# Attention in front of a SiLU layer: full-array scores with zero-padded keys, values for four heads in 32-column tiles, q in 128 partitions

## The chip, the cores and the metric

The kernel runs on one core of a Trainium2 chip. The metric is device time in microseconds (us), the median of several executions of the same program. An execution counts as fast when it lies within 1.5% of the fastest of its kernel. Unless it says otherwise, everything below compares fast runs.

## The reference

Keys and values are averaged over groups of 8 positions, then ordinary attention is computed, and its result is fed to a two-layer network with SiLU.

```python
B, H, S, D = 8, 8, 576, 64                       # q, k, v, float32
k_p = k.reshape(B, H, 72, 8, D).mean(axis=3)      # 72 pooled keys
v_p = v.reshape(B, H, 72, 8, D).mean(axis=3)
attn = softmax(q @ k_p^T / sqrt(D))               # 576 x 72 per head
x = (attn @ v_p) as (4608 tokens, 512)
out = silu(x @ w_in) @ w_out                      # 512 -> 2048 -> 512
```

The inputs are drawn at 0.1 (q, k, v), so a score is a few thousandths and the softmax is nearly flat. That matters for one experiment below.

## The kernel before

There are nine passes of 512 tokens ("iterations" t). Each is `up` (64 matmuls into hp_ps, then SiLU) and `down` (64 matmuls into o_ps). The attention of batch t+1 is woven between the matmuls of iteration t. A "visit" is one pair of heads and half of the queries: two score matmuls, the exponential, two matmuls for the sums (den), two for the values (nu).

```python
# scores: 64 rows per head, the two heads on the two row halves
for s in range(2):
    rows = slice(s * D, (s + 1) * D)
    nc.tensor.matmul(sc_ps[:, s, :HS], lhsT=st["kT"][rows, p, :],
                     rhs=st[f"qT{p}"][rows, cols], start=True, stop=True)
# ... exponential on ScalarE ...
# sums and values: 64 columns per head
for s in range(2):
    nc.tensor.matmul(den_ps[s*D:(s+1)*D, :HS], lhsT=ones, rhs=es[:, s, :], ...)
for s in range(2):
    nc.tensor.matmul(nu_ps[s*D:(s+1)*D, :HS], lhsT=st["vp"][:, 2*p+s, :], rhs=es[:, s, :], ...)
# ... 1/den as exp(-ln(den)) on ScalarE ...
# xT is written with a step of 6 bf16 elements
dst = xT[:, p, b*S:(b+1)*S].rearrange("d (q j) -> d j q", j=QJ)
nc.vector.tensor_mul(out=dst[:, f*HJ:(f+1)*HJ, :], in0=nu_ps..., in1=rec...)

# loads: q in 96 partitions, k and v in 72; all on SyncE's queue
q_src = q[b].rearrange("h (p j) d -> p h (j d)", j=QJ)      # QJ = 6
k_src = k[b].rearrange("h (sp p) d -> sp h (p d)", p=POOL)
# ... weights on GpSimd's queue: w_in in 4 loads, then w_out in 4 loads
for c in range(NC):
    nc.gpsimd.dma_start(out=w_in_sb[:, :, cs], in_=w_in_r[:, :, cs])
```

Of the kernel before, what the change touches and what calls it, by code (L numbers as in the profile page):

```python
# [27 lines left out]
FP32 = mybir.dt.float32  # L28
FP32R = mybir.dt.float32r
BF16 = mybir.dt.bfloat16  # L30
# [6 lines left out]
def kernel(  # L37
# [9 lines left out]
    nc = tc.nc  # L47

    B, H, S, D = q.shape
    POOL = 8  # L50
    SP = S // POOL
# [8 lines left out]
    QP = 96  # L60
    QJ = S // QP
    HS = S // 2
    HJ = QJ // 2
    score_scale = float(1.0 / (D ** 0.5) / POOL)
    assert NT == B + 1 and NP == KF

    w_in_r = moe_w_in.rearrange("(kt kp) f -> kp kt f", kp=128)
    w_out_r = moe_w_out.rearrange("(kt kp) d -> kp kt d", kp=128)

# [10 lines left out]
    ones = singles.tile([SP, D], BF16, name="ones")  # L80
# [3 lines left out]

    batches = {}

    def load_batch(b, parts):
        st = batches.setdefault(b, {})
        k_raw = big.tile([SP, H, POOL * D], FP32, tag="k_raw", name="k_raw")
        q_raw = big.tile([QP, H, QJ * D], FP32, tag="q_raw", name="q_raw")  # L90
        v_raw = big.tile([SP, H, POOL * D], FP32, tag="v_raw", name="v_raw")
        st.update(k_raw=k_raw, q_raw=q_raw, v_raw=v_raw)
        k_src = k[b].rearrange("h (sp p) d -> sp h (p d)", p=POOL)
        v_src = v[b].rearrange("h (sp p) d -> sp h (p d)", p=POOL)
        q_src = q[b].rearrange("h (p j) d -> p h (j d)", j=QJ)
        hp = H // parts
        for i in range(parts):
            hs = slice(i * hp, (i + 1) * hp)
            nc.sync.dma_start(out=k_raw[:, hs, :], in_=k_src[:, hs, :])
            nc.sync.dma_start(out=q_raw[:, hs, :], in_=q_src[:, hs, :])  # L100
        for i in range(parts):
            hs = slice(i * hp, (i + 1) * hp)
            nc.sync.dma_start(out=v_raw[:, hs, :], in_=v_src[:, hs, :])

    def cast_q(b, parts):
        st = batches[b]
        q_bf = big.tile([QP, NP, QJ, 2, D], BF16, tag="q_bf", bufs=1, name="q_bf")
        st["q_bf"] = q_bf
        hp = H // parts
        for i in range(parts):  # L110
            for p in range(i * hp // 2, (i + 1) * hp // 2):
                for s in range(2):
                    nc.gpsimd.tensor_copy(  # L113
                        out=q_bf[:, p, :, s, :],
                        in_=st["q_raw"][:, 2 * p + s, :].rearrange(
                            "q (j d) -> q j d", d=D
                        ),
                    )

    def pool_kv(b, which, parts):  # L120
        st = batches[b]
        raw = st[f"{which}_raw"]
        dst = mid.tile([SP, H, D], BF16, tag=f"{which}p", name=f"{which}p")
        st[f"{which}p"] = dst
        hp = H // parts
        for i in range(parts):
            hs = slice(i * hp, (i + 1) * hp)
            w = POOL * D // 2
            while w > D:
                nc.vector.tensor_add(  # L130
                    out=raw[:, hs, :w], in0=raw[:, hs, :w], in1=raw[:, hs, w : 2 * w]
                )
                w //= 2
            nc.vector.tensor_add(  # L134
                out=dst[:, hs, :], in0=raw[:, hs, :D], in1=raw[:, hs, D : 2 * D]
            )

    def k_transpose(b):
        st = batches[b]
        kT_ps = psum.tile([128, NP, SP], BF16, tag="mm", bufs=3, name="kT_ps")  # L140
        for p in range(NP):
            nc.tensor.transpose(  # L142
                kT_ps[:, p, :],
                st["kp"][:, 2 * p : 2 * p + 2, :].rearrange("s h d -> s (h d)"),
                ident[:SP, :SP],
            )
        kT = mid.tile([128, NP, SP], BF16, tag="kT", name="kT")
        nc.vector.tensor_copy(out=kT, in_=kT_ps)
        st["kT"] = kT

    def q_transpose(b, p):
        st = batches[b]
        qT_ps = psum.tile([128, QJ, QP], BF16, tag="mm", bufs=3, name="qT_ps")
        for j in range(QJ):
            nc.tensor.transpose(  # L155
                qT_ps[:, j, :],
                st["q_bf"][:, p, j, :, :].rearrange("q s d -> q (s d)"),
                ident[:QP, :QP],
            )
        qT = mid.tile([128, S], BF16, tag=f"qT{p}", bufs=1, name="qT")  # L160
        nc.vector.tensor_copy(out=qT, in_=qT_ps.rearrange("d j q -> d (j q)"))  # L161
        st[f"qT{p}"] = qT

    def scores(b, p, f):
        st = batches[b]
        cols = slice(f * HS, (f + 1) * HS)
        sc_ps = psum.tile([SP, 2, 512], FP32, tag="sc", bufs=1, name="sc_ps")
        for s in range(2):
            rows = slice(s * D, (s + 1) * D)
            nc.tensor.matmul(  # L170
                sc_ps[:, s, :HS],
                lhsT=st["kT"][rows, p, :],
                rhs=st[f"qT{p}"][rows, cols],
                start=True, stop=True,
            )
        es = mid.tile([SP, 2, HS], BF16, tag="es", bufs=3, name="es")
        nc.scalar.activation(es, sc_ps[:, :, :HS], func=AF.Exp, scale=score_scale)  # L177
        st[f"es{p}{f}"] = es

    def values(b, p, f):  # L180
        st = batches[b]
        es = st.pop(f"es{p}{f}")
        nu_ps = psum.tile([128, 512], FP32, tag="nd", bufs=3, name="nu_ps")
        den_ps = psum.tile([128, 512], FP32, tag="nd", bufs=3, name="den_ps")
        for s in range(2):
            nc.tensor.matmul(  # L186
                den_ps[s * D : (s + 1) * D, :HS],
                lhsT=ones, rhs=es[:, s, :], start=True, stop=True,
            )
        for s in range(2):  # L190
            nc.tensor.matmul(  # L191
                nu_ps[s * D : (s + 1) * D, :HS],
                lhsT=st["vp"][:, 2 * p + s, :], rhs=es[:, s, :],
                start=True, stop=True,
            )
        lnd = mid.tile([128, HS], FP32, tag="lnd", name="lnd")
        nc.scalar.activation(lnd, den_ps[:, :HS], func=AF.Ln)  # L197
        rec = mid.tile([128, HS], FP32, tag="rec", name="rec")
        nc.scalar.activation(rec, lnd, func=AF.Exp, scale=-1.0)  # L199
        dst = xT[:, p, b * S : (b + 1) * S].rearrange("d (q j) -> d j q", j=QJ)  # L200
        nc.vector.tensor_mul(  # L201
            out=dst[:, f * HJ : (f + 1) * HJ, :],
            in0=nu_ps[:, :HS].rearrange("d (j q) -> d j q", q=QP),
            in1=rec.rearrange("d (j q) -> d j q", q=QP),
        )
# [37 lines left out]
    def down(t, h_T, fillers):  # L243
        nm = NTT // 128
        step = spread(fillers, nm * KG)
        for m in range(nm):
# [11 lines left out]
            r0 = t * NTT + m * 128  # L258
            nc.sync.dma_start(out=out[r0 : r0 + 128, :], in_=o_sb)
# [4 lines left out]
    load_batch(0, 2)  # L264
# [3 lines left out]
    cast_q(0, 2)  # L268
    NC = 4
    for c in range(NC):  # L270
        cs = slice(c * d_ff // NC, (c + 1) * d_ff // NC)
        nc.gpsimd.dma_start(out=w_in_sb[:, :, cs], in_=w_in_r[:, :, cs])  # L272
    for c in range(NC):
        cs = slice(c * KG // NC, (c + 1) * KG // NC)
        nc.gpsimd.dma_start(out=w_out_sb[:, cs, :], in_=w_out_r[:, cs, :])  # L275
    load_batch(1, 1)
    pool_kv(0, "k", 2)
    k_transpose(0)
    for p in range(NP):
        q_transpose(0, p)  # L280
    pool_kv(0, "v", 2)
    seq = [(p, f) for p in range(NP) for f in range(2)]
    for n, (p, f) in enumerate(seq):
        scores(0, p, f)
        if n:
            values(0, *seq[n - 1])
    values(0, *seq[-1])

    for t in range(NT):
        a = t + 1  # L290
        f_up, f_down = [], []
        if a < B:
            if a + 1 < B:
                f_up.append((0, lambda: load_batch(a + 1, 1)))
            f_up.append((0, lambda: cast_q(a, 1)))
            f_up.append((0, lambda: pool_kv(a, "k", 1)))
            f_up.append((22, lambda: k_transpose(a)))
            for p in range(NP):
                f_up.append((26 + 6 * p, lambda p=p: q_transpose(a, p)))
            f_up.append((50, lambda: pool_kv(a, "v", 1)))  # L300
            f_down.append((0, attn_tables))
            for n, (p, f) in enumerate(seq):
                f_down.append((6 * n + 1, lambda p=p, f=f: scores(a, p, f)))
                f_down.append((6 * n + 6, lambda p=p, f=f: values(a, p, f)))
        moe_tables()
        h_T = up(t, f_up)
        down(t, h_T, f_down)
# [30 lines left out]
```

## Time and profile before

| | before |
|---|---|
| median, lowest and highest of 3 runs | 364.18 us, 363.87 to 366.18 |
| profiled execution | 362.77 us, span of the core 360.9 us |
| one iteration with attention | 36.4 us |
| last wait for w_out ends | 65.35 us |
| second iteration starts | 83.61 us |

The page's groups show two rows that the change aims at and one that it does not. In each row come line, engine, operation, outputs and inputs, shapes and count, then busy us and mean ns of one, then idle time before them and what ended it. The first line is SyncE's DMA queue: packets, MB, busy share of 16 engines over the span.

```profile
q1 hardware_dynamic: 20904, 37.75, 38.6%
...
L250 PE MATMUL o_ps<-w_out_sb,h_T 128*128 128x512 bf16 x576 | 148.4, 387 | 10.8 <-DMA w_out_sb<-in_moe_w_out_dram 10.8
...
L201 DVE TENSOR_TENSOR xT<-nu_ps,rec 128x288 bf16<-128x288 f32 x64 | 71.4, 1124 | 77.3 <-ACT rec L199 77.2
```

TensorE waits 10.8 us for w_out, all of it at the start. The multiply that writes xT takes 1124 ns because of its stepped output, or so the change supposes.

How fast the first loads come in, the table of windows tells. Its columns are the window, its length, busy us (and count) of TensorE, its weight loads, VectorE, ScalarE and GpSimd, the granted clock, the DMA share and GB/s.

```profile
4.00:8.00 4.00, 0.00 (x0) 0.00 (x0) 1.91 (x2) 0.00 (x0) 0.00 (x0) 1.00 1.06 264
...
12.00:16.00 4.00, 2.42 (x28) 2.10 (x29) 3.13 (x8) 0.00 (x0) 2.77 (x5) 1.00 1.04 265
```

The DMA engines are full (the share adds up the time of packets, which overlap, so it can pass 1.0) and move 264 GB/s. Keep the second figure in mind: a full share does not tell the rate.

### The profile page before, as it was taken

To read this page: it belongs to the slowest core of one execution; us is meant where nothing else is said; L and a number is where in the kernel's file an instruction comes from. 1 tells how busy PE (TensorE), PEld (TensorE's weight loads), DVE (VectorE), ACT (ScalarE), POOL (GpSimd) and SP (SyncE) were. 2 spreads that over 40 slices of the span, in tenths; PEclk is the share of its full clock that TensorE was granted. 3 is DMA by queue.
4 is the path that set the end of the run, shared out by engine and by line. 5 is a ranking of instruction groups with operands and counts; after the bars stand their busy time and mean duration, and the time that the engine had idled before them with its cause. 6 is when DMAs were issued, how large, how long until landed. Compare 5 with 4: busy or idle time off the path is not lost.

```text
span 360.9 us, 4481 instructions
## 1 busy us (share of the span) xinstructions
PE 323.2 (90%) x1760; PEld 136.3 (38%) x1760; DVE 176.5 (49%) x194; ACT 197.2 (55%) x353; POOL 38.1 (11%) x79
## 2 busy tenths in 40 slices
PE   0378855799999999999999999999999999999995
PEld 0232411234433443345334533453345334444442
DVE  2698421366646664665467546754675463011011
ACT  1186541365676567656765676567655765622610
POOL 1633204000030004000400040004000000000000
PEclk9999985699999999999999999999999999999999
DMA  7999988105950595059414941495110011011002
GB/s 193 244 248 259 259 208 214 50 30 156 200 125 31 146 203 131 30 146 207 116 44 131 210 114 57 121 209 122 62 58 2 0 58 60 0 54 64 0 29 87
DMA packets 25148, 42.22 MB, mean 117 GB/s; under 512 B 1064, under 2 KB 11304, under 8 KB 25128
## 3 DMA queue, kind: packets, MB, share of 16 engines
q1 hardware_dynamic: 20904, 37.75, 38.6%
q0 software_dynamic: 4224, 4.19, 6.9%
q8 instruction: 13, 0.21, 0.3%
q14 instruction: 7, 0.06, 0.1%
HBM read 36.70 MB, written 9.44 MB: 128 GB/s over the span
## 4 chain that ended last, share of the span: by engine, by line
PE 76%; DMA 16%; ACT 4%; POOL 2%; SPq 0%; issue 0%; DVE 0%
PE o_ps L250 35%; PE hp_ps L230 31%; DMA w_out_sb<-in_moe_w_out_dram 12%; PE den_ps L186 4%; PE sc_ps L170 3%; DMA q_raw<-in_q_dram 3%; ACT L208 2%; PE nu_ps L191 2%; PE qT_ps L155 2%; ACT es L177 1%; ACT h_T L237 1%; POOL w_in_sb L272 1%; POOL w_out_sb L275 1%; POOL q_bf L113 1%; PE kT_ps L142 0%
## 5 line engine op out<-in xcount | busy, mean ns | idle before, releaser
L250 PE MATMUL o_ps<-w_out_sb,h_T 128*128 128x512 bf16 x576 | 148.4, 387 | 10.8 <-DMA w_out_sb<-in_moe_w_out_dram 10.8
L230 PE MATMUL hp_ps<-xT,w_in_sb 128*128 128x512 bf16 x576 | 134.5, 385 | 1.5 <-DMA w_in_sb<-in_moe_w_in_dram 1.0
L237 ACT ACTIVATE h_T<-hp_ps 128x512 bf16<-128x512 f32 x144 | 86.0, 597 | 76.3 <-PE hp_ps L230 76.3
L201 DVE TENSOR_TENSOR xT<-nu_ps,rec 128x288 bf16<-128x288 f32 x64 | 71.4, 1124 | 77.3 <-ACT rec L199 77.2
L250 PEld LDWEIGHTS <-h_T 128*128 128x128 bf16 x576 | 51.5, 98 | 77.0 <-issue 21.2
L230 PEld LDWEIGHTS <-w_in_sb 128*128 128x128 bf16 x576 | 54.7, 99 | 64.0 <-issue 4.4
L257 DVE COPY o_sb<-o_ps 128x512 f32<-128x512 f32 x36 | 27.1, 752 | 59.8 <-PE o_ps L250 59.7
L113 POOL CAST q_bf<-q_raw 96x384 bf16<-96x384 f32 x64 | 31.3, 533 | 211.1 <-DMA q_raw<-in_q_dram 178.7
L197 ACT ACTIVATE lnd<-den_ps 128x288 f32<-128x288 f32 x64 | 26.2, 409 | 49.8 <-PE den_ps L186 49.8
L177 ACT ACTIVATE es<-sc_ps 72x576 bf16<-72x576 f32 x64 | 40.4, 631 | 17.2 <-PE sc_ps L170 17.1
L130 DVE TENSOR_TENSOR k_raw<-k_raw 72x1024 f32<-72x1024 f32 (+2 forms) x18 | 28.4, 1579 | 9.0 <-DMA k_raw<-in_k_dram 8.7
L199 ACT ACTIVATE rec<-lnd 128x288 f32<-128x288 f32 x64 | 28.3, 443 | 2.4 <-DVE xT L201 0.4
L161 DVE COPY qT<-qT_ps 128x576 bf16<-128x576 bf16 x32 | 14.6, 457 | 29.1 <-PE qT_ps L155 29.1
L130 DVE TENSOR_TENSOR v_raw<-v_raw 72x1024 f32<-72x1024 f32 (+2 forms) x18 | 28.3, 1572 | 0.4
L186 PE MATMUL den_ps<-es,ones 72*64 72x288 bf16 x128 | 21.5, 329 | 5.8 <-ACT es L177 4.7
L170 PE MATMUL sc_ps<-qT,kT 64*72 64x288 bf16 x128 | 21.5, 331 | 0.9 <-ACT es L177 0.7
L191 PE MATMUL nu_ps<-es,vp 72*64 72x288 bf16 x128 | 20.4, 310 | 1.7 <-DVE vp L134 0.9
L186 PEld LDWEIGHTS <-ones 72*64 72x64 bf16 x128 | 8.2, 110 | 35.7 <-issue 33.9
L155 PEld LDWEIGHTS <-q_bf 96*128 96x128 bf16 x192 | 12.2, 103 | 6.8 <-POOL q_bf L113 0.2
L142 PE MATMUL kT_ps<-ident,kp 72*128 72x72 bf16 x32 | 2.7, 206 | 13.3 <-DVE kp L134 13.3
L170 PEld LDWEIGHTS <-kT 64*72 64x72 bf16 x128 | 7.6, 111 | 17.7 <-issue 17.5
L155 PE MATMUL qT_ps<-ident,q_bf 96*128 96x96 bf16 x192 | 14.0, 215 | 0.0
(16 smaller groups left out, 52.6 us busy)
## 6 DMA issues: line engine op xcount, KB each, us to landing
out_dram<-o_sb SPq DMA_DIRECT2D x36, 256.0 KB
k_raw<-in_k_dram SPq DMA_DIRECT2D x7, 1152.0 KB
q_raw<-in_q_dram SPq DMA_DIRECT2D x7, 1152.0 KB
v_raw<-in_v_dram SPq DMA_DIRECT2D x7, 1152.0 KB
w_in_sb<-in_moe_w_in_dram POOLq DMA_DIRECT2D x4, 512.0 KB, 19.0
w_out_sb<-in_moe_w_out_dram POOLq DMA_DIRECT2D x4, 512.0 KB, 38.1
k_raw<-in_k_dram SPq DMA_DIRECT2D x2, 576.0 KB
q_raw<-in_q_dram SPq DMA_DIRECT2D x2, 576.0 KB
```

Source lines behind the costliest of these rows:

```text
L113: nc.gpsimd.tensor_copy(out=q_bf[:, p, :, s, :], in_=st["q_raw"][:, 2 * p + s, :].rearrange("q (j d) -> q j d", d=D),)
L130: nc.vector.tensor_add(out=raw[:, hs, :w], in0=raw[:, hs, :w], in1=raw[:, hs, w : 2 * w])
L155: nc.tensor.transpose(qT_ps[:, j, :], st["q_bf"][:, p, j, :, :].rearrange("q s d -> q (s d)"), ident[:QP, :QP],)
L170: nc.tensor.matmul(sc_ps[:, s, :HS], lhsT=st["kT"][rows, p, :], rhs=st[f"qT{p}"][rows, cols], start=True, stop=True,)
L177: nc.scalar.activation(es, sc_ps[:, :, :HS], func=AF.Exp, scale=score_scale)
L186: nc.tensor.matmul(den_ps[s * D : (s + 1) * D, :HS], lhsT=ones, rhs=es[:, s, :], start=True, stop=True,)
L191: nc.tensor.matmul(nu_ps[s * D : (s + 1) * D, :HS], lhsT=st["vp"][:, 2 * p + s, :], rhs=es[:, s, :], start=True, stop=True,)
L199: nc.scalar.activation(rec, lnd, func=AF.Exp, scale=-1.0)
L201: nc.vector.tensor_mul(out=dst[:, f * HJ : (f + 1) * HJ, :], in0=nu_ps[:, :HS].rearrange("d (j q) -> d j q", q=QP), in1=rec.rearrange("d ( ...
L230: nc.tensor.matmul(hp_ps, lhsT=w_in_sb[:, kk, g * 128 : (g + 1) * 128], rhs=xT[:, kk, t * NTT : (t + 1) * NTT], start=(kk == 0), stop=(kk ...
L237: nc.scalar.activation(h, hp_ps, func=AF.Silu)
L250: nc.tensor.matmul(o_ps, lhsT=h_T[g][:, m * 128 : (m + 1) * 128], rhs=w_out_sb[:, g, :], start=(g == 0), stop=(g == KG - 1),)
```

## The change

A matmul here uses all 128 rows of TensorE's array or some of them, and 128, 72, 64 or 32 columns ("64*72" in the views is 64 rows and 72 columns); going from one such shape to another is called a switch below. The intent is to take switches of the array's tile shape out of the attention, to halve ScalarE's work on the sums, and to make the xT write contiguous. For the last, q is laid out so that the token order of xT is permuted and the output transfer puts it right. Parts without a bearing are cut.

```diff
 # scores: the keys of the other head are zeros, so all 128 rows are used
-                lhsT=st["kT"][rows, p, :],
-                rhs=st[f"qT{p}"][rows, cols],
+                lhsT=kz[b % 2][:, 2 * p + s, :],
+                rhs=st["qT"][:, p, cols],
 # values: four heads at once, 32 columns each
+        for hh in range(4):
+                den_ps[32 * hh : 32 * (hh + 1), :HS], lhsT=ones, rhs=es[hh // 2][:, hh % 2, :]
+        for c in range(2):
+            for hh in range(4):
+                    nu_ps[32 * hh : 32 * (hh + 1), :HS],
+                    lhsT=st["vp"][:, 4 * g + hh, 32 * c : 32 * (c + 1)], ...
+        for c in range(2):
+            nc.vector.tensor_mul(out=xT[:, 2 * g + c, cols], in0=nu[c][:, :HS], in1=rec)
 # q: heads 0-3 in partitions 0-63, heads 4-7 in 64-127, two transfers
-        q_src = q[b].rearrange("h (p j) d -> p h (j d)", j=QJ)
+        for g in range(2):
+            nc.sync.dma_start(out=q_raw[64 * g : 64 * (g + 1), :, :],
+                in_=q[b, 4 * g : 4 * (g + 1)].rearrange("h (p i) d -> p h (i d)", i=QI))
 # k and v of batches 0 and 1: k in partitions 0-63, v in 64-127 of one buffer
+            for half, src in ((0, k), (64, v)):
+                nc.sync.dma_start(out=raw[half : half + 64, ii, :], in_=...[:, ii, :])
 # w_in in 16 pieces of 32 partitions (rows permuted to match xT)
+        for hh in (0, 2, 1, 3):
+            for c32 in range(2):
+                nc.gpsimd.dma_start(out=w_in_sb[32 * hh : 32 * (hh + 1), c32::2, cs], ...)
 # output: two transfers of 64 rows for each tile instead of one of 128
+            for u in range(2):
+                nc.sync.dma_start(out=out_r[n // QI, n % QI], in_=o_sb[64 * u : 64 * (u + 1), :])
# [cut: k, v of batches 2 to 7 stay in 72 partitions, one buffer each; tree adds; transposes]
```

> **What bounds the kernel now.** I read the slices of the page first, then the chain of work that ended last, then the waits, and last the timeline of one steady iteration. The slices (40 of 9.0 us each):
>
> ```profile
> PE   0378855799999999999999999999999999999995
> PEclk9999985699999999999999999999999999999999
> DMA  7999988105950595059414941495110011011002
> ```
>
> There are two regimes. In slices 0 to 6 (to 63 us) the DMA engines are full and TensorE is not; from slice 7 on TensorE is 90% busy or more at full clock. The chain, in order of time, agrees:
>
> ```profile
> 20.45 44.87 DMA w_out_sb<-in_moe_w_out_dram
> 65.35 0.58 PE o_ps L250
> ...
> 83.61 4.96 PE hp_ps L230 x23
> ...
> 120.00 4.96 PE hp_ps L230 x23
> ...
> 156.39 4.96 PE hp_ps L230 x23
> ...
> 301.93 13.81 PE hp_ps L230 x64
> ```
>
> So the last quarter of w_out lands at 65.35 us and TensorE has waited for it; after that the chain stays on TensorE. "hp_ps x23" starts each iteration of 512 tokens: 83.61, 120.00, 156.39 and so on to 301.93, six iterations of 36.4 us. The last two have no attention and take 13.81 us per 64 matmuls, 0.216 us each, 27.6 us an iteration. **Attention therefore costs 36.4 - 27.6 = 8.8 us of TensorE per iteration.** How, the TensorE timeline of one visit (a pair of heads, 288 queries) shows; columns are start, length, engine, line and operation:
>
> ```profile
> 138.48 0.31 PE L170 MATMUL sc_ps<-qT,kT 64*72 64x288 bf16 x2
> 138.73 1.25 PE L250 MATMUL o_ps<-w_out_sb,h_T 128*128 128x512 bf16 x5
> 139.91 0.31 PE L186 MATMUL den_ps<-es,ones 72*64 72x288 bf16 x2
> 140.06 0.29 PE L191 MATMUL nu_ps<-es,vp 72*64 72x288 bf16 x2
> 140.28 0.39 PE L250 MATMUL o_ps<-w_out_sb,h_T 128*128 128x512 bf16 x1
> 140.60 0.31 PE L170 MATMUL sc_ps<-qT,kT 64*72 64x288 bf16 x2
> ```
>
> Read starts, not lengths (lengths overlap). Five o_ps from 138.73 need 5 x 0.216 = 1.08, to 139.81; den starts at 139.91, 0.10 later. One o_ps from 140.28 ends at 140.50; sc starts at 140.60, again 0.10 later. Two den take 0.15 to the next start, two nu 0.22, two sc 0.25. A matmul of 288 columns at the rate of the 512-column ones is 0.12 us, so two den or two sc in different parts of the array run together, and the rest is switching. A visit costs 0.10 + 0.15 + 0.22 + 0.10 + 0.25 = 0.82 us; the period, 2.12 us between the two sc, minus six o_ps (1.30), gives 0.82 too. Eight visits: 6.6 us. The other 2.2 us: 24 q transposes at 6 per 0.26 us (1.04), k transposes (0.14), one wait at the first den for the ScalarE table load and exponential (0.78), edges of the first visit (0.25). Around the q transposes (96 rows by 128 columns) no 0.10 gap shows: six hp_ps from 126.39 take 1.30 and the transposes follow at 127.68.
>
> **What the Trainium skill says.** "TensorEngine Tiling (Array Packing)", Key Properties: changing the tiling mode drains TensorE, and tiles work independently. The trace agrees: 0.10 us before each change to half-array tiles, and two tiles in the time of one. The same page, Tiling Modes, has four 128 by 32 tiles; no run here shows these yet. "TensorE: Matmul & The Clock Gate", LDWEIGHTS, gives a load as the number of columns over 1.2 per ns: four loads of 32 columns take as long as two of 64, about 107 ns by that page, below the 0.12 us stream. "DMA: Bandwidth & Descriptors", Issuing engines are not separate DMA queues: loads issued by different engines share the 16 DMA engines. The trace agrees: with w and q/k/v in flight (20 to 40 us) the DMA share is 1.16 and neither queue runs ahead.
>
> **The change, part by part.**
>
> *Scores* use all 128 rows, the other head's rows being zero. Two no longer run together (2 x 0.12 = 0.24), but nothing switches: 0.25 per pair and no 0.10. Eight pairs save 8 x 0.10 = 0.8 us per iteration.
>
> *Values* handle four heads: four den, four nu, four nu, each group in one stream if 32-column tiles overlap as the 64-column ones do: 0.10 + 0.15 + 0.15 + 0.22 = 0.62 us, four times, 2.5 us; before, 8 x (0.10 + 0.15 + 0.22) = 3.8 us. Saved: 1.3 us.
>
> *q transposes*: 18 of 128 columns (0.056 us each by the same rate) for 24 at 0.043: 1.0 for 1.04. Nothing gained.
>
> Sum: 2.1 us per iteration; over six, **12.6 us**, all on the chain, since TensorE ends those stages. The 0.78 us wait stays: the first exponential must now free sc_ps before the second pair of scores, at about the same place.
>
> *Off the chain*: the xT multiply (1124 ns, 64 of them) writes with a step of 12 bytes; now it is contiguous. A VectorE add of 256 columns takes 421 ns, so I estimate 0.45 us and 43 us less VectorE work. ScalarE does half of the Ln and Exp(-): 32 x (0.41 + 0.44) = 27 us less. Neither bounds the steady stage (VectorE is busy 10.5 of 17.6 us in one down phase, ScalarE 11.2), so I count nothing there. One cost: the last values now stand 11 o_ps before the next iteration instead of 15, 0.86 us less slack, where the last multiply ended at 155.0 and hp started at 156.2. That fits, barely; I allow 0.2 us per iteration, **1.2 us**.
>
> *Start.* The limit is bytes: batches 0, 1, 2 (3 x 3.54 MB) and 8.4 MB of weights all pass before 63.5 us, and the change loads the same three batches and weights. Two things shift. First, the w_in issue follows q's cast: q alone comes first (1.18 MB, the same amount that let the first cast start at 8.3 us before), four casts of about 0.7 us (533 ns for 384 columns, now 576), so w_in issues from some 11 us instead of 15.2. Second, rows get longer: k and v of batches 0 and 1 go from 2 KB to 6 KB and 18 KB, q from 1.5 to 2.3 KB, w_in from 1 to 2 KB as written. The q/k/v queue took 38.6% of 16 x 360.9 us for 20904 packets, 107 ns each for 1.8 KB. If a quarter of that is per packet, about 3 to 4 us of the first 62 go. So I put the last w_out quarter at 61 us, 4 us earlier. After it the first iteration has three visits of scores left and four of values at the new prices: 1.6 us less. **Start: 5.6 us.**
>
> *End.* Each output tile leaves in two transfers of 64 rows: one more issue at about 0.4 us after the last tile: **+0.4 us**.
>
> Sum: 364.2 - 12.6 + 1.2 - 5.6 + 0.4 = 347.6 us.
>
> **Rivals.** (1) *32-column tiles do not overlap four ways.* At 0.25 us per group, values cost 0.10 + 0.25 + 0.25 + 0.32 = 0.92 us four times, 3.7 us, and nothing of the 1.3 us is left: about 356 us. For it: twice as many weight loads per microsecond, and loads of 64 and 72 columns show 110 ns against 98 for 128. Against: two tiles overlap fully now. (2) *The start gets longer.* GpSimd now issues w_in in 16 pieces with eight in flight at most; w_out, then the cast of batch 1's q, stand behind them, and the transposes of batch 1 behind that cast. Batch 0's scores also wait for all of k and v to be loaded, added and transposed before the first (before, k alone: the first scores at 15.9 us). If up(0) starts at 40 us instead of 28.75, it still ends near 57, before w_out; a further 6 us of delay would show: 353 us or so. Large rows of k and v may also crowd out the weights, moving w_out back to 64. (3) *A wait takes the place of the switches*: with one buffer for scores and three banks for den, nu, nu, TensorE may wait for ScalarE or VectorE. Per values step ScalarE needs 2 x 0.64 + 0.41 + 0.44 = 2.1 us and the step lasts 13 x 0.216 + 1.1 = 3.9 us, so I see room; the banks come free about 2.3 us after den. (4) *Nothing happens*, because transfers hide it: against this stands a DMA share below 0.6 after slice 9 and a chain without DMA there.
>
> **Range and chances.** The steady saving is well supported (8 to 14 us), the start less so (-3 to +9 us). That spans about 340 to 356. Slower would need both rival 1 and a start 10 us worse. Faster by over 2% means below 356.9 us.
>
> **What would show it.** Iterations from hp to hp of 34.3 to 34.5 us; no gap before sc; den to nu to nu 0.15 us apart with x4; xT multiply near 0.45 us; the last w_out wait ending near 61 us and the second iteration's first hp_ps near 78 us. The prediction is wrong if den groups stand 0.25 us apart or more, if gaps before hp_ps name the xT multiply, if q_bf or k and v of batch 1 hold TensorE in the first up phase, or if w_out lands after 65 us.

## The result

| | before | after |
|---|---|---|
| median of 4 runs (lowest to highest) | 364.02 us (363.29 to 366.18) | 350.55 us (348.99 to 351.98) |
| profiled execution | 362.77 us | 351.98 us |
| span of the core in the profile | 360.9 us | 350.2 us |

All runs are fast ones. The ratio is 0.9619, with a 95% interval of 0.9561 to 0.9677. A ratio here and below is the mean time of one kernel's fast runs over that of the other's in the same rounds, so it is not quite the ratio of the medians.

The profiles are of a quick execution of the kernel before and of the slowest of the four of the kernel after, so they differ by 10.7 us in span where the medians differ by 13.5.

The page after: slices of 8.76 us each, then the queue and the groups that answer to those of before.

```profile
PE   0336878499999999999999999999999999999994
...
PEclk9999989679999999999999999999999999999999
DMA  7999999612866296628653964496420021022022
...
q1 hardware_dynamic: 17808, 37.76, 47.2%
...
L319 PE MATMUL o_ps<-w_out_sb,h_T 128*128 128x512 bf16 x576 | 142.9, 385 | 6.1 <-DMA w_out_sb<-in_moe_w_out_dram 6.1
...
L272 DVE TENSOR_TENSOR xT<-nu_ps,rec 128x288 bf16<-128x288 f32 x64 | 26.3, 453 | 98.8 <-ACT rec L270 87.5
```

The xT multiply fell from 1124 to 453 ns, as wanted. But read the queue line: the same 37.7 MB in fewer packets (17808 for 20904) kept the engines busy for longer. Before, 38.6% of 16 x 360.9 us is 2229 engine-us, 107 ns for a packet of 1.81 KB; after, 47.2% of 16 x 350.2 us is 2645 engine-us, 149 ns for one of 2.12 KB. Fewer and longer packets cost 19% more engine time. And slice 7, near 65 us, still stands at 4 tenths of TensorE.

The chain of work that ended last, in order of time, columns start, length, what:

```profile
43.73 25.22 DMA w_out_sb<-in_moe_w_out_dram
68.99 1.01 PE o_ps L319 x2
...
86.73 4.53 PE hp_ps L299 x21
...
120.64 4.53 PE hp_ps L299 x21
...
290.19 13.81 PE hp_ps L299 x64
```

Between 86.73 and 290.19 lie six iterations of 33.91 us (before, 36.39). The last w_out wait ends at 68.99 instead of 65.35, and the second iteration starts at 86.73 instead of 83.61. The last two iterations take 55.29 us in both kernels. After the last copy of an output tile come 4.0 us instead of 3.0. In the profiles, then: start +3.1, six iterations 203.5 - 218.3 = -14.9, tail +1.0; together -10.7.

One visit after, on TensorE:

```profile
138.48 1.46 PE L319 MATMUL o_ps<-w_out_sb,h_T 128*128 128x512 bf16 x6
139.87 0.31 PE L252 MATMUL den_ps<-es,ones 72*32 72x288 bf16 x4
140.00 0.42 PE L260 MATMUL nu_ps<-es,vp 72*32 72x288 bf16 x8
140.35 0.39 PE L319 MATMUL o_ps<-w_out_sb,h_T 128*128 128x512 bf16 x1
140.58 0.41 PE L235 MATMUL sc_ps<-qT,kz 128*72 128x288 bf16 x2
140.82 1.46 PE L319 MATMUL o_ps<-w_out_sb,h_T 128*128 128x512 bf16 x6
```

Six o_ps from 138.48 end at 139.78; den starts 0.10 later, the one gap before a group of small matmuls that is left. Four den take 0.13 to the next start and eight nu 0.35. The o_ps at 140.35 runs its 0.22 and sc starts without a gap. A visit of four heads and half the queries thus costs 0.10 + 0.13 + 0.35 for values and 2 x 0.245 for scores, 1.07 us, four times 4.3 us; before it was 8 x 0.82 = 6.6 us.

### The profile page after: what moved, and what is told of

The parts are those of the page before. It is cut to its first block, busy times and chain, and to the rows that moved or that the text cites. A ratio compares the mean times of both kernels' runs of the same rounds, so it can differ in the third digit from the quotient of the medians.

```text
span 350.2 us, 4636 instructions
## 1 busy us (share of the span) xinstructions
PE 308.6 (88%) x1858; PEld 146.0 (42%) x1858; DVE 137.3 (39%) x204; ACT 177.3 (51%) x299; POOL 50.3 (14%) x61
## 3 DMA queue, kind: packets, MB, share of 16 engines
q1 hardware_dynamic: 17808, 37.76, 47.2%
## 4 chain that ended last, share of the span: by engine, by line
PE 74%; DMA 17%; ACT 4%; POOL 1%; issue 1%; SPq 0%; DVE 0%; POOLq 0%
PE o_ps L319 33%; PE hp_ps L299 32%; DMA w_in_sb<-in_moe_w_in_dram 8%; DMA w_out_sb<-in_moe_w_out_dram 7%; PE sc_ps L235 4%; ACT L277 2%; DMA q_raw<-in_q_dram 2%; PE nu_ps L260 2%; PE den_ps L252 2%; PE qT_ps L121 2%; ACT es L242 1%; ACT h_T L306 1%; POOL q_bf L109 1%; POOL w_out_sb L361 0%; PE kT_ps L165 0%
## 5 line engine op out<-in xcount | busy, mean ns | idle before, releaser
L272 DVE TENSOR_TENSOR xT<-nu_ps,rec 128x288 bf16<-128x288 f32 x64 | 26.3, 453 | 98.8 <-ACT rec L270 87.5
L109 POOL CAST q_bf<-q_raw 128x576 bf16<-128x576 f32 x32 | 37.0, 1196 | 167.0 <-PE qT_ps L121 118.6
L145 DVE TENSOR_TENSOR raw<-raw 72x2048 f32<-72x2048 f32 (+1 forms) x24 | 44.8, 1868 | 0.4
L235 PE MATMUL sc_ps<-qT,kz 128*72 128x288 bf16 x128 | 28.5, 307 | 7.7 <-ACT es L242 7.7
L268 ACT ACTIVATE lnd<-den_ps 128x288 f32<-128x288 f32 x32 | 13.1, 410 | 31.8 <-PE den_ps L252 31.8
L127 DVE COPY qT<-qT_ps 128x640 bf16<-128x640 bf16 (+1 forms) x32 | 14.5, 458 | 35.1 <-PE qT_ps L121 35.1
L121 PE MATMUL qT_ps<-ident,q_bf 128*128 128x128 bf16 x144 | 14.1, 233 | 12.8 <-POOL q_bf L109 12.7
L235 PEld LDWEIGHTS <-kz 128*72 128x72 bf16 x128 | 15.4, 122 | 21.5 <-issue 12.3
L260 PE MATMUL nu_ps<-es,vp 72*32 72x288 bf16 x256 | 14.8, 311 | 0.5 <-ACT lnd L268 0.5
L270 ACT ACTIVATE rec<-lnd 128x288 f32<-128x288 f32 x32 | 14.2, 445 | 1.0
```

The lines of the kernel that those rows point to most:

```text
L109: nc.gpsimd.tensor_copy(out=q_bf[:, a, :, s, :], in_=st["q_raw"][:, 2 * a + s, :].rearrange("q (i d) -> q i d", d=D),)
L121: nc.tensor.transpose(qT_ps[:, i, :], st["q_bf"][:, a, i0 + i, :, :].rearrange("q s d -> q (s d)"), ident,)
L145: nc.vector.tensor_add(out=raw[:, :, :w], in0=raw[:, :, :w], in1=raw[:, :, w : 2 * w])
L235: nc.tensor.matmul(sc_ps[:, s, :HS], lhsT=kz[b % 2][:, 2 * p + s, :], rhs=st["qT"][:, p, cols], start=True, stop=True,)
L260: nc.tensor.matmul(nu_ps[32 * hh : 32 * (hh + 1), :HS], lhsT=st["vp"][:, 4 * g + hh, 32 * c : 32 * (c + 1)], rhs=es[hh // 2][:, hh % 2, :] ...
L272: nc.vector.tensor_mul(out=xT[:, 2 * g + c, cols], in0=nu[c][:, :HS], in1=rec)
```

## The experiments

Eleven kernels ran, in three groups that each shared their runs of the kernel before. Its medians were 363.59, 364.19 and 363.84 us.

### The steady stage, part by part

**Scores on half rows again.** Everything else stays as after the change.

```diff
-                lhsT=kz[b % 2][:, 2 * p + s, :],
-                rhs=st["qT"][:, p, cols],
+                lhsT=kz[b % 2][s * D : (s + 1) * D, 2 * p + s, :],
+                rhs=st["qT"][s * D : (s + 1) * D, p, cols],
```

> Changed kernel with the scores back on half the rows of the array (64 rows of the same keys and queries); all else as changed, result correct. Theory (what the full-array scores save is the switch of tiling mode before each pair): every sc start stands 0.10 us after the end of the o_ps before it again, eight times per iteration, so an iteration goes from 33.9 to 34.7 us and the whole is 5 to 6 us longer than the changed kernel. Rival (the saving per iteration comes from the values alone): iteration stays at 33.9 us, total within 1 us of the changed kernel.

Measured: 356.03 us (354.86 to 356.29), ratio to before 0.9799 (0.9777 to 0.9822), results correct. An iteration takes 34.55 us, 0.64 more than after the change. The visit on TensorE:

```profile
139.99 0.39 PE L319 MATMUL o_ps<-w_out_sb,h_T 128*128 128x512 bf16 x1
140.31 0.31 PE L235 MATMUL sc_ps<-qT,kz 64*72 64x288 bf16 x2
```

The o_ps runs from 139.99 to 140.21 and sc starts at 140.31: the gap of 0.10 is back, though the same matmuls with 128 rows had none. Seven of the eight pairs show it; at the eighth, which waits for the first exponential, the wait shrinks from 0.67 to 0.57 us instead. So the scores' share is the gap, 0.08 for each of eight pairs on average.

**Values of two heads on 64-column tiles.** Eight visits again, `ones` 64 wide; w_in in four plain loads, because xT has its old row order.

```diff
-        for hh in range(4):
-                den_ps[32 * hh : 32 * (hh + 1), :HS], ...
+        for s in range(2):
+                den_ps[s * D : (s + 1) * D, :HS], ...
-    visits = [(f, g) for f in range(2) for g in range(2)]
+    seq = [(p, f) for f in range(2) for p in range(NP)]
+                f_down.append((6 * n + 1, lambda p=p, f=f: scores(a, p, f)))
+                f_down.append((6 * n + 6, lambda p=p, f=f: values(a, p, f)))
# [cut: the value matmuls and the multiply for one pair; w_in as in the next experiment]
```

> Changed kernel with the values of two heads at a time on 64-column tiles, eight times per iteration, and w_in in four loads in plain row order (the row order that this layout needs); result correct. Theory: values cost 8 x 0.47 = 3.8 us per iteration instead of 4 x 0.58 = 2.3, so an iteration takes 35.3 to 35.4 us (33.9 + 1.45); against the run with plain w_in alone the total is 9 to 11 us longer. Rival (the merging of visits gives nothing beyond the scores): iteration below 34.5 us.

Measured: 359.02 us (358.49 to 359.69), ratio 0.988 (0.9858 to 0.9902), correct. An iteration takes 35.46 us, 1.55 more than with 32-column tiles. The total is 7.5 us above the kernel with the same w_in loads (the next experiment), less than the 9 to 11 expected: in the profiles its start came 2.5 us earlier, which took back part of 6 x 1.55 = 9.3. Scores and values together give 0.64 + 1.55 = 2.19 of the 2.48 us that an iteration gained. The rest, about 0.3, was not separated by a run; in the trace the wait for the first exponential is 0.67 us instead of 0.78, the transposes 1.13 instead of 1.18 and the edges 0.19 instead of 0.25.

### What holds the start: two theories that fell

**Is it the issue of w_in in 16 pieces?** GpSimd issues w_out only at 39.1 to 43.7 us after the change, at 18.3 to 20.4 before. With w_in in four plain loads its rows are wrong on purpose.

```diff
-    w_in_r = moe_w_in.rearrange("(g hh c dd) f -> hh c dd g f", g=2, hh=4, c=2)
+    w_in_r = moe_w_in.rearrange("(kt kp) f -> kp kt f", kp=128)
-        for hh in (0, 2, 1, 3):
-            for c32 in range(2):
-                nc.gpsimd.dma_start(out=w_in_sb[32 * hh : 32 * (hh + 1), c32::2, cs], ...)
+        nc.gpsimd.dma_start(out=w_in_sb[:, :, cs], in_=w_in_r[:, :, cs])
# [cut: NC = 4 and the four calls]
```

> Changed kernel with w_in loaded in four transfers of 128 partitions in plain row order instead of 16 of 32 partitions; the rows of w_in are then in the wrong order, so the result is wrong on purpose. Theory A (the w_in pieces, eight in flight at most, hold back the issue of w_out): w_out is issued by 20 us instead of 39 to 44, its last quarter lands at 58 to 63 us instead of 69, the second iteration starts at 77 to 81 instead of 86.7, total 6 to 10 us below the changed kernel. Theory B (the long rows of k and v and the total bytes set the landing): last w_out still after 66 us, total within 2 us of the changed kernel.

Measured: 351.49 us (350.83 to 352.72), ratio 0.9676 (0.9649 to 0.9702); relative error 1.205, as intended. w_out was issued at 14.4 to 16.6 us, 25 us sooner, and the last quarter still landed only at 69.3 us (69.0 after the change); the second iteration started at 86.28. Here a transfer in full queues was not sooner for being issued sooner. The theory fell.

**Is it the long rows of k and v?** Batches 0 and 1 take the 72-partition layout of the kernel before.

```diff
-    FLAT = 2
-    load_kv_flat(0, 3)
+    FLAT = 0
+    load_kv(0)
-            raw = big.tile([SP, H, POOL * D], FP32, tag=f"{name}_raw", bufs=1, name="raw")
+            raw = big.tile([SP, H, POOL * D], FP32, tag=f"{name}_raw", bufs=2, name="raw")
# [cut: adds and transposes of batch 0 in the same layout]
```

> Changed kernel with k and v of batches 0 and 1 loaded in the 72-row layout of all other batches (2 KB rows, two buffers each) instead of 64-partition halves with 6 and 18 KB rows; w_in still in 16 pieces; result correct. Theory A (issue of w_in pieces): w_out issue stays late (after 35 us) and the second iteration starts within 2 us of 86.7. Theory B (long rows crowd out the weights): DMA in 4 to 24 us rises from 223 to some 255 GB/s, the last w_out lands 3 to 6 us earlier, total 3 to 6 us below the changed kernel.

Measured: 349.1 us (348.08 to 350.13), ratio 0.9607 (0.9577 to 0.9636), correct: no different from the change as a whole. The rate did not rise, it fell, to 133 GB/s in 8 to 12 us and 158 in the next window. The window, then from the chain what held the path instead, a single piece of 41 us:

```profile
8.00:12.00 4.00, 1.02 (x9) 0.88 (x9) 0.27 (x1) 0.00 (x0) 2.35 (x4) 1.00 1.09 133
```

```profile
9.49 41.08 DMA raw<-in_k_dram
```

The keys of batch 1 landed only at 50.6 us and held up the first `up`. The last quarter of w_out landed at 67.8 us, hardly earlier than after the change, but TensorE came to it later still and did not wait. It is a trade of one late load for another, and no support for long rows as the cause.

### What holds the start: q in one transfer of 128 partitions or in two of 64

**q in one transfer of 128 partitions.** The same bytes with the same rows of 2.3 KB on the same queue. The heads come out paired wrongly, on purpose.

```diff
-        for g in range(2):
-            nc.sync.dma_start(out=q_raw[64 * g : 64 * (g + 1), :, :],
-                in_=q[b, 4 * g : 4 * (g + 1)].rearrange("h (p i) d -> p h (i d)", i=QI))
+        nc.sync.dma_start(out=q_raw,
+            in_=q[b].rearrange("(m g) (p i) d -> (g p) m (i d)", g=2, i=QI))
```

> Changed kernel with each batch of q loaded in one transfer of 128 partitions (rows of 2304 bytes as before) instead of two of 64; the heads then pair wrongly, so the result is wrong on purpose. Theory C (transfers that fill only 64 partitions at a time move slower): the first cast of q starts at some 7.5 us instead of 9.0, and with q a third of the q/k/v bytes the last w_out lands 2 to 3 us earlier (66 us instead of 69), total 1 to 3 us below the changed kernel. Rival D (row length or the order of rows in memory sets the rate): first cast at 9.0 us again, total unchanged.

Measured: 347.52 us (344.66 to 348.05), ratio 0.9523 (0.9469 to 0.9577); every run lies below every run of the kernel after. The comparison with the reference passed all the same: with a softmax this flat, queries of the wrong head hardly change the result, so it can't vouch for the pairing. The windows of after, then of this kernel:

```profile
3.00:6.00 3.00, 0.00 (x0) 0.00 (x0) 0.00 (x0) 0.00 (x0) 0.00 (x0) 1.00 1.07 242
...
12.00:16.00 4.00, 1.17 (x10) 0.64 (x7) 2.96 (x7) 0.00 (x0) 3.77 (x8) 1.00 1.02 223
```

```profile
3.00:6.00 3.00, 0.00 (x0) 0.00 (x0) 0.00 (x0) 0.00 (x0) 0.00 (x0) 1.00 1.09 411
...
12.00:16.00 4.00, 0.50 (x3) 0.23 (x3) 2.85 (x7) 0.00 (x0) 1.33 (x3) 1.00 1.03 219
```

The DMA share is the same 1.07 to 1.09 in the first window of both, yet it moves 411 GB/s instead of 242, most of it q. In the later window, where k and v still arrive in 64-partition pieces, nothing changed. The first cast of q starts at 6.52 us instead of 8.97, the last w_out wait ends at 63.66 and the second iteration starts at 79.40. That profile is of the fastest of the four runs, 2.9 us below their median, so some 3 of those 7 us are this run's luck. Two things changed together, though: the partitions that one transfer spans, and the number of transfers. No run separates them.

The Trainium skill advises the same: "DMA: Bandwidth & Descriptors", Rules for kernel authors, asks for 128 partitions and at least 1 MiB a transfer for full bandwidth, and says of two transfers to disjoint partition halves "Don't bother — they serialize". This case's trace agrees for q, 411 against 242 GB/s.

**The halves on two queues.** If a 64-partition transfer leaves half of something idle, its other half beside it on another queue should fill it.

```diff
-            nc.sync.dma_start(
+            eng = nc.scalar if (g == 1 and b < 2) else nc.sync     # q
+            eng.dma_start(
-                nc.sync.dma_start(
+                eng = nc.scalar if half else nc.sync               # v
+                eng.dma_start(
```

> Changed kernel with the upper halves of the first two batches (q heads 4 to 7, and v) issued on the ScalarE queue, the lower halves on SyncE as now: the same transfers, but both halves of the partitions are filled at the same time; result correct. Theory C: DMA in 4 to 20 us rises from 213-224 to 255 GB/s or more, last w_out 4 to 7 us earlier, total 4 to 7 us below the changed kernel. Rival D (each row costs what it costs): rate stays below 230 GB/s, total within 1.5 us.

Measured: 348.94 us (348.4 to 349.22), ratio 0.9576 (0.9537 to 0.9615), correct. k and v sped up: 252, 281 and 286 GB/s in the three windows from 8 to 20 us, where after the change all three have 223 to 224. The one in which k and v move almost alone:

```profile
12.00:16.00 4.00, 1.32 (x11) 1.06 (x12) 3.52 (x9) 0.00 (x0) 4.00 (x8) 1.00 1.04 281
```

q's halves did not speed up, 222 GB/s in 4 to 8 us. But they did not move side by side either: up to 4.25 us the trace has packets of ScalarE's queue alone (202 of them, 0.47 of that half's 0.59 MB), and SyncE's half followed. So for q this run did not test what it was meant to test. The last w_out wait ended at 66.61, 2.4 us earlier than after the change, the second iteration began at 83.50, 3.2 us earlier, and the total is 1.6 us below, where 4 to 7 was expected.

That q is faster as one transfer of 128 partitions is shown. The mechanism is not. A limit of some 220 GB/s for one half of the partitions would fit the 213 to 224 with one half at a time, and leave room for 281 with k and v side by side and 411 with q over all 128. That is only a reading of these figures, and the 133 GB/s of the 72-partition loads above does not follow from it.

### What holds the start: loads that nobody needs yet

Batch 2 is first used in the second iteration, but is asked for in the first, ahead of the last weights. **Here its k goes into the buffer of batch 1's k and v**, so that the load has to wait for batch 1's additions, and q and v stand behind it.

```diff
+            if b == 2 and name == "k":
+                raw = big.tile([128, KI, POOL * D], FP32, tag="kv_raw", bufs=1, name="kv_raw")[:SP, :H, :]
-            if a + 1 < B:
+            if a + 1 < B and t > 0:
                 f_up.append((0, lambda: load_q(a + 1)))
+                if t == 0:
+                    f_up.append((51, lambda: load_q(a + 1)))
```

> Changed kernel with the loads of batch 2 (3.54 MB) held back until batch 1's k and v have been added (its k goes into their buffer, v and q stand behind it in the queue); result correct. Theory E (w_out's landing is set by all the bytes that are queued before it at some 216 GB/s): w_out lands before 58 us, no TensorE wait for it is left, the second iteration starts at 77 to 79 us instead of 86.7, total 7 to 10 us below the changed kernel. Rival (the weights queue is slow by itself, by issue or by its casts): w_out still later than 64 us, total within 3 us.

Measured: 342.73 and 339.44 us in the two fast runs, correct; two more, 344.59 and 344.62, lie over 1.5% above the fastest and were not counted, so there is no ratio with an interval. All four are below every run of the kernel after. Batch 2 was issued at 46.12 us, TensorE waited 2.4 us for w_out instead of 6.1, and the second iteration began at 77.51 (expected 77 to 79). From the chain:

```profile
40.83 19.86 DMA w_out_sb<-in_moe_w_out_dram
...
77.51 4.53 PE hp_ps L302 x21
```

The theory held for the total and the second iteration. For w_out it was too hopeful: the last quarter landed at 60.7 us, not before 58, and a wait was left.

**The same for the kernel before**, by one buffer for its k and v:

```diff
-        k_raw = big.tile([SP, H, POOL * D], FP32, tag="k_raw", name="k_raw")
+        k_raw = big.tile([SP, H, POOL * D], FP32, tag="k_raw", bufs=1, name="k_raw")
# [the same for v_raw]
```

> Kernel before, with one buffer each for the raw k and v instead of two, so that each batch's k and v wait for the adds of the batch before (batch 2's k then waits until 34 us or so); result correct. Theory E: w_out's last quarter lands 3 to 8 us earlier than 65.3 us and the total falls by as much (356 to 361 us). Rival (held-back loads of later iterations now come too late and TensorE waits for k): total equal or longer, with a wait for k_raw or k's transposes in each iteration.

Measured: 363.83 us (363.03 to 364.73), ratio 0.9987 (0.9943 to 1.0031), correct, the same. But the lever did not grip: batch 2's k was issued at 35.5 us, q at 35.9 and v at 47.5, and the kernel before had held those three back till 27.7, 36.2 and 44.5 us already. It decides nothing.

### A repeat, and both causes taken away

The third group ran the kernel after once more, unchanged, as a base.

> The changed kernel itself once more, for comparison with the two repaired versions on the same chip. Every theory: 349 to 352 us, iterations of 33.9 us, second iteration from 85 to 88 us.

Measured: 351.07 us (349.43 to 352.54), ratio 0.9647 (0.9612 to 0.9681); last w_out wait to 67.79, second iteration at 85.92. The start moves by about a microsecond from run to run.

**q in one 128-partition load with the right pairing, and batch 2 late.** The heads' order is carried through the keys and the exponentials, at the price of one add cut into two smaller ones for each of batches 2 to 7 and four more copies each for batches 0 and 1. As the flat softmax hides a wrong pairing, the order was followed through the index expressions by hand: pair 2a+g, half s, holds head 4a+2s+g in q, in the keys and in the values alike.

```diff
-        dst = st["qT"].rearrange("d (g a) (i p) -> d a i g p", g=2, p=64)
+        dst = st["qT"].rearrange("d (a g) (i p) -> d a i g p", g=2, p=64)
-                lhsT=ones, rhs=es[hh // 2][:, hh % 2, :], start=True, stop=True,
+                lhsT=ones, rhs=es[hh % 2][:, hh // 2, :], start=True, stop=True,
# [cut: q's single load and the late batch 2 as above; keys written as "(a g s)"]
```

> Changed kernel with both repairs of the start: q in one transfer of 128 partitions, with the heads paired so that the result is right (two more small VectorE adds per batch), and batch 2's loads held back until batch 1's k and v have been added. Theory (the start was lost to transfers of 64 partitions and to bytes queued ahead of w_out; with w_out no longer last, the path is k and v of batch 0, its attention, and the first up phase): first cast of q at 6.5 us, second iteration at 74.5 to 76.5 us instead of 77.5 with the late loads alone, total 340 to 342.5 us. Rival (the first up phase waits for something else, such as the cast of batch 1's q or the half clock): second iteration at 77 us or later, total as with the late loads alone, 343 to 344 us.

Measured: 337.13 us (336.55 to 337.31), ratio to before 0.9262 (0.9247 to 0.9277), correct within the limit said. It beats both kernels, the one after by 13.9 us of the medians of the same group. From its page and its chain:

```profile
PEclk9999999999999999999999999999999999999999
...
q1 hardware_dynamic: 17680, 37.75, 45.0%
```

```profile
38.61 18.08 DMA w_out_sb<-in_moe_w_out_dram
...
71.94 4.53 PE hp_ps L313 x21
```

The clock never drops now; after the change it stood at 0.50 to 0.70 from 64 to 76 us, behind the waits for w_out. From 68 to 76 us TensorE was busy for 3.66 us at 0.50 and 4.00 us at 0.70; at full clock that work would take some 3 us less (an estimate), so the clock is part of the gain. The last w_out wait is 0.2 us, and q's first window again moves 412 GB/s. The second iteration starts at 71.94 and the total is 337.13, both better than the 74.5 to 76.5 and 340 to 342.5 expected.

**The same with v on ScalarE's queue:**

> As the run with both repairs, and v of batches 0 and 1 issued on the ScalarE queue, so that the lower and upper halves of the k and v buffer fill at the same time. Theory (halves filled at the same time move at 280 GB/s instead of 220, as the two-queue run showed for k and v but not for q): the last add of batch 0's k and v starts 1.5 to 2.5 us earlier, the second iteration 1 to 2.5 us earlier, total 338 to 341 us. Rival (the time is then set elsewhere in the start): within 0.7 us of the run with both repairs.

Measured: 340.56 us (340.34 to 341.14), ratio 0.9363 (0.9345 to 0.9382), correct: 3.4 us worse than without it, and a miss, though the total lies within the 338 to 341 expected: that range had been set for a slower base. v now runs beside q, which is needed first; the first cast starts at 12.23 us and the second iteration at 75.21. The gain on k and v was real in the experiment where q was split too, but here it is paid for by q.

## Why the prediction was right or wrong

The total held, 350.55 us against 347.6 and inside the range, because the steady stage gave more than the prediction asked and the start gave nothing. That these two misses, 3.5 us more and 6.0 us less, partly cancel is luck. Of the four signs that the prediction named for being wrong, two came: w_out landed after 65 us, and q_bf of batch 1 held TensorE in the first `up`.

1. **What bounds the kernel: right.** The chain stays on TensorE through all six iterations, and each part put back by itself showed up in the iteration's length. Two readings of the page were off. TensorE is at 90% and full clock from slice 8, not 7, and slices 6 and 7 stand at 5 and 6 tenths of the clock, which the prediction left out of the start. And the DMA share is not "below 0.6 after slice 9": slices 10, 14 and others show 9 tenths. What speaks against rival 4 is the chain without DMA.
2. **Scores, 0.8 us an iteration: right in kind.** Half rows cost 0.64 more, and the trace shows it as the gap before sc.
3. **Values, 1.3 us: right in kind, a little small.** Two heads on 64-column tiles cost 1.55 more. Four 32-column matmuls do overlap: 0.13 us for four, where 0.15 was predicted. Rival 1 is refuted: a weight load of 32 columns took about as long (94 to 101 ns) as one of 128 (99), but twice as many of them did not show.
4. **q transposes, nothing: right**, 0.05 us.
5. **0.2 us less slack an iteration: not needed.** No wait for xT shows in the steady stage; the multiply's 453 ns, predicted as 0.45, leaves room. So the iteration gained 2.48 us and not 1.9; six of them 14.9, not 11.4.
6. **The start, 5.6 us to be gained: wrong.** In the profiles it lost 3.1 us. By medians it neither lost nor gained much: if the iterations and the tail are taken from the profiles, the total of -13.5 less -14.9 for the iterations and +1.0 for the tail leaves +0.4. The step that failed is "rows get longer ... If a quarter of that is per packet, about 3 to 4 us of the first 62 go", and from it "I put the last w_out quarter at 61 us". It came at 69.0 (67.8 in the repeat). The estimate took a quarter of a packet's time as a cost per packet without a row of the trace that shows it. The trace of the kernel before had one: from 10.5 to 11.4 us only q's 1.5 KB rows move, 98 ns each, and from 8.3 to 9.4 us almost only the 2 KB rows of k and v, 128 ns each. That leaves about 8 ns per packet (an estimate; the two also differ in partitions). After the change the longer packets took 149 ns for 107. What the runs put in its place: q's two halves moved 242 GB/s where one transfer of 128 partitions moved 411, with equal rows, and batch 2's bytes stood ahead of w_out; held back, w_out landed at 60.7. The earlier issue of w_in was the second leg of that step. It came as predicted, at 11.4 us, and did not bear either: w_out was issued later, behind the 16 pieces, and issuing it 25 us sooner changed nothing.
7. **The tail, +0.4: too small**, 1.0 us measured for the two output transfers of 64 rows a tile.
8. **Rival 2, a longer start, came true in part.** Its last clause, large rows of k and v crowding out the weights, named the place rightly: w_out was late. But the crowd was batch 2 and slow halves. The first `up` began at 37.2 us instead of 28.75, close to the 40 of the rival, and as it says there it still ended before w_out. GpSimd's order did cost something, a wait of 2.42 us for q_bf of batch 1, yet w_out landed later than all that.

Still open is whether q's gain comes from the 128 partitions or from being one transfer, and why the loads of k and v in 72 partitions fell to 133 GB/s in the changed kernel, when the kernel before moved such loads at 208 (8.3 to 9.4 us).

## What to carry to other kernels

A full DMA share is not a full rate: read GB/s beside it, and try a load as one transfer over all 128 partitions before counting row lengths. When the start is bound by loads, ask first what is loaded there that nobody needs yet; issuing the needed load sooner did nothing here. Before a cost per packet goes into a sum, look for two stretches of the trace with packets of different size. On TensorE, count changes of tile shape: at 0.10 us each, zero padding that makes a small matmul full-sized can be the cheaper form.

## What the Trainium skill lacked or had wrong

- "TensorEngine Tiling (Array Packing)" says that a change of tiling mode drains TensorE, but I found no figure for it there: here 0.10 us before each change to half-row or column tiles, and none when the scores used all rows. For its four 128 by 32 tiles these runs show 0.13 us for four matmuls of 288 columns.
- "DMA: Bandwidth & Descriptors" says of two transfers to partition halves "Don't bother — they serialize". That was not the whole of it: halves of k and v issued from two engines moved 252 to 286 GB/s, from one engine 223 to 224.
- I found no page with a measured time for a VectorE multiply that writes bf16 with a step of 12 bytes: 1124 ns for 128 x 288 here, and 453 ns contiguous.
